# A cached-attention and MLP block on one core: wider filler matmuls, the first head's values on GpSimd's DMA queue, and a last output tile in three column parts

## The chip, the cores and the metric

The kernel runs on one core of one Trainium2 chip. The metric is the device time of one execution in microseconds, lower is better. The number for the kernel before is the median of six runs.

## The reference, cut to what matters

The input x has 2048 rows (tokens) of 640 columns. There are 32 heads with cached keys and values of 2048 positions and 128 columns each, all in bfloat16.

```python
mod = silu(c) @ w_mod                 # six vectors of 640: sa, ca, ga, sb, cb, gb
h   = layernorm(x) * (1 + ca) + sa
q   = h @ wq                          # 32 heads of 128
p   = softmax(q @ k_cache.T / sqrt(128))
x   = x + ga * ((p @ v_cache) @ wo)
h   = layernorm(x) * (1 + cb) + sb
u   = gelu(layernorm(h) @ w1)         # four column groups, shifted by +1, -1, +2, -2 rows
x1  = h + shifted(u) @ w2
h2  = gelu(layernorm(x1) @ w3) @ w4   # 1728 hidden columns
out = x + gb * (x1 + h2)
```

## The kernel before, in words

The tokens are cut into four chunks of 512 and the heads into eight groups of four. Attention is 128 steps. A step takes one chunk and one head: 16 score matmuls of 128x512 (L806), eight exponentials on ScalarE of 128x1024 each (L808), and 64 matmuls of 128x129 against the values (L825, the 129th column sums the exponentials). While a step runs, TensorE also makes the next step's queries (`q_proj`, L729), and after four heads of a chunk it multiplies by wo (`wo_group`, L760). Then a tail does the MLP in tiles: `w1_part` (L940), `w2_tile` (L963), `w3_part` (L989) and `w4_tile` (L1002 and after). The order of the tail is written out by hand in the list `TAIL`. Its last entry is D15, `w4_tile` of the last 128 rows.

The order of instructions on each engine is made by a planner in Python (class `Plan`). Each operation has a cost in nanoseconds, a priority, and the operations that it depends on. TensorE follows the priorities strictly. The other engines are filled by the planner's clock. `after=` gives only an order in the planner; the program has no wait for it. `reads` and `writes` become semaphore waits. The planner's own figures are not times of the chip.

Before the first step there is a head of some 13 us:

- POOL fills `ones` (L403) and an identity, and the 129th columns of five value buffers (`v_ones`, L410).
- SP loads the row c, two tiles of x, three of the five parts of w_mod's first 1280 columns (`wm[0]`, `wm[2]`, `wm[4]`, L434) and the first head's slice of wq. ACT's queue loads the other two tiles of x, `wm[1]` and `wm[3]`, and, later, another slice of wq.
- TensorE runs filler matmuls on `ones` (`spin` and `dummy`, L440): 30, then it turns c into a column (`spread`, L452), then 26 more. Then come 5 times 10 matmuls of one column (`mcol`, L465), one set per part of w_mod, which give sa and ca. In the first two sets a filler follows each matmul.
- The four normalised tiles of x are turned by TensorE (L586), scaled by ca and sa into `hT` on DVE (L595, k = 0, 2, 4) and ACT (L590, k = 1, 3), and multiplied by wq (L729). Three more groups of fillers (8, 9 and 9) lie around this.
- The first head's keys K0 come by four transposing DMAs on SP (L610); the first waits for `wm[0]`, the others for `wm[2]`. The first head's values V0 come in two halves of 256 KB on ACT's queue (L677), which the planner puts behind the second pair of small activations, L504 and L505. POOL's queue then brings the second chunk of x (L562, it waits for the first `hT` of ACT), a slice of wq (L619, it waits for the second exponential) and the values V1, V2, V3 (L616; V1 waits for the third exponential).

At the end, `w4_tile` of D15 makes two halves of 320 columns: 14 matmuls, a multiplication by gb and an addition on DVE, and an output DMA for each half. The first half's outputs leave while the second half is computed.

Each engine's program ends in a second block of instructions, `fast`, that is reached by a branch. DVE takes its last six operations there and SP its last five (`FIRST`).

Of the kernel before, what the change touches and what calls it, by code (L numbers as in the profile page):

```python
# [6 lines left out]
ACT = mybir.ActivationFunctionType  # L7
# [33 lines left out]
class Plan:  # L41
# [50 lines left out]
    def schedule(self):  # L92
        for o in self.ops:
            for d in o.need:
                o.deps[d()] = True
            pre = set(o.deps) | o.order
            for d in pre:
                d.succ.append(o)
            o.ndep = len(pre)
        t_eng = {e: 0.0 for e in self.ENG}  # L100
        dma_t = {e: 1600.0 for e in self.ENG}
        avail = {e: [] for e in self.ENG}
        for o in self.ops:
            if o.ndep == 0:
                avail[o.eng].append(o)
        self.seq = {e: [] for e in self.ENG}
        free = {p: [] if p in self.late else [(0.0, b, ()) for b in range(len(bk))] for p, bk in self.pools.items()}
        left = {t: len(t.refs) for o in self.ops for t in o.newps}
        self.busy = {e: 0.0 for e in self.ENG}
        self.all = []  # L110
        pe = sorted((o for o in self.ops if o.eng == "PE"), key=lambda o: (o.prio, o.seq))
        pe_i = 0
        port = {"POOL": 0.0, "DVE": 0.0}
        while len(self.all) < len(self.ops):
            best = None
            for e in self.ENG:
                st = []
                for o in avail[e]:
                    if e == "PE" and o is not pe[pe_i]:
                        continue  # L120
                    r = o.ready
                    if not all(free[t.pool] for t in o.newps):
                        continue
                    r = max([r] + [min(free[t.pool])[0] for t in o.newps])

                    x = port["POOL" if e == "DVE" else "DVE"] if o.dual else 0.0
                    st.append((max(r, t_eng[e], x), o.prio, o.seq, o))
                if not st:
                    continue
                lim = min(st)[0] + 30.0  # L130
                c = min((x for x in st if x[0] <= lim), key=lambda x: x[1:3])
                if best is None or c[0] < best[0]:
                    best = c
            assert best is not None, ("stuck", pe[pe_i].prio, [d.eng for d in pe[pe_i].deps if not hasattr(d, "end")])
            s, o = best[0], best[3]
            e = o.eng
            avail[e].remove(o)
            if e == "PE":
                pe_i += 1
            for t in o.newps:  # L140
                b = min(free[t.pool])
                free[t.pool].remove(b)
                t.bank, t.ap = b[1], self.pools[t.pool][b[1]]
                for d in b[2]:
                    o.deps.setdefault(d, False)
            o.start = s
            if o.dual:
                port[e] = s + o.dur
            t_eng[e] = s + (o.dur if o.dma else max(o.dur - self.LAP.get(e, 0.0), 60.0))
            self.busy[e] += o.dur  # L150
            if o.dma:
                t = max(dma_t[e], s + o.dur)
                both = min(max(0.0, max(dma_t[x] for x in self.ENG if x != e) - t), o.kb * 1024 / 190.0)
                dma_t[e] = t + both + (o.kb * 1024 - 190.0 * both) / 380.0
                o.end = dma_t[e] + 2000.0
            else:
                o.end = s + o.dur + o.lat
            o.idx = len(self.seq[e])
            self.seq[e].append(o)
            self.all.append(o)  # L160
            for pool, bank in o.gives:
                free[pool].append((o.end, bank, (o,)))
            for u in o.succ:
                u.ndep -= 1
                u.ready = max(u.ready, (o.start if o not in u.deps else t_eng[e] + 45.0 if e == u.eng and e != "PE" and not o.dma and not u.deps[o] else o.end) + u.slack - (45.0 if e == u.eng and e in self.LAP and not o.dma else 0.0) + (1500.0 if o.dma and u.eng in ("DVE", "ACT") and not u.dma else 0.0))
                if u.ndep == 0:
                    avail[u.eng].append(u)
            for t in o.ptiles:
                left[t] -= 1
                if left[t] == 0:  # L170
                    last = {}
                    for r in t.refs:
                        if r.eng not in last or r.idx > last[r.eng].idx:
                            last[r.eng] = r
                    free[t.pool].append((max(r.end for r in t.refs), t.bank, tuple(last.values())))
        self.total = max(o.end for o in self.ops)
# [103 lines left out]
def fast_path(nc, es, flag, A_x, A_k_cache, A_v_cache, A_wq, A_wo, B_w1, B_w2, B_w3, B_w4, c, w_mod, out):  # L280
    _, SQ, D = A_x.shape
# [3 lines left out]
    KT, NKT, HD, QC, NC = D // 128, SK // 128, D // 2, 512, SQ // 512  # L285
    NF = (FF + 127) // 128
# [15 lines left out]
    P = Plan()  # L302
    T = lambda ap=None: Tile(ap)
# [24 lines left out]
    mod_t = {p: sb("mod%d" % p, [128, D], F32) for p in (2, 3, 4, 5)}  # L328
# [67 lines left out]
    def dma(eng, fn, kb, reads, writes, prio, need=(), after=(), over=()):  # L396
        return P.op(eng, fn, {"SP": 480, "ACT": 480, "POOL": 1000}[eng], reads, writes, prio, dma=True, kb=kb, need=need, after=after, over=over)
# [39 lines left out]

    def dummy(e, n, t=None):
        for _ in range(n):
            ins = e.matmul((t or warm)[:, 0:128], ones_t[:], ones_t[:], start=True, stop=True)  # L440
        return ins

    def spin(n, key, pool=None):
        t = Tile(pool=pool) if pool else warm
        P.op("PE", lambda e: dummy(e, n, t), n * 56, (ones,), (t,), key)

    mc, c_ps = Tile(pool="M"), Tile(pool="M")
    spin(30, -300)

    def spread(e):  # L450
        for k in range(KT):
# [6 lines left out]
    P.op("DVE", lambda e: e.reciprocal(c_e.ap, c_e.ap), 190, (c_e,), (c_e,), -300)  # L458
    P.op("DVE", lambda e: e.tensor_mul(out=c_f.ap, in0=c_e.ap, in1=c_ps[:, 0:KT]), 170, (c_e, c_ps), (c_f,), -300)
    P.op("DVE", lambda e: e.tensor_copy(s_bf.ap, c_f.ap), 170, (c_f,), (s_bf,), -300)  # L460
    spin(26, -298)
    for k in range(KT):
        def mcol(e, k=k):
            for j in range(2 * KT):
                ins = e.matmul(mc[:, j:j + 1], wm_ap[:, k, j * 128:(j + 1) * 128], s_bf[:, k:k + 1],  # L465
                               start=(k == 0 and j == 0), stop=(k == KT - 1), skip_group_check=True)
                if k < 2:
                    dummy(e, 1)
            return ins
        P.op("PE", mcol, 2 * KT * (85 if k < 2 else 62), (wm[k], s_bf, ones), (mc,) + ((warm,) if k < 2 else ()), -290 + k, accum=True)  # L470
    saT, caT = T(small(KT)), T(small(KT))
    P.op("DVE", lambda e: e.tensor_copy(saT.ap, mc[:, 0:KT]), 170, (mc,), (saT,), -290)
    P.op("DVE", lambda e: e.tensor_scalar_add(out=caT.ap, in0=mc[:, KT:2 * KT], scalar1=1.0), 170, (mc,), (caT,), -290)
# [200 lines left out]
            dma("SP", lambda e, n=n, p=p: e.dma_start(mod_t[p][:], m_scr.ap()[n:n + 1, :].to_broadcast([128, D])), 320, lines, tuple(mod[p]), slot + 1.0)  # L674

    for a, z, t in ((0, NKT // 2, v0a), (NKT // 2, NKT, V[0])):
        dma("ACT", lambda e, a=a, z=z: e.dma_start(V_ap[0][:, a:z, 0:128], A_v_cache[0, 0, a * 128:z * 128].rearrange("(t p) d -> p t d", p=128)),  # L677
            256, (), (t,), -296.5, after=(ln0[1],))

    def load_head(h):  # L680
# [103 lines left out]
    def step(s):  # L784
# [3 lines left out]
        q = QT[s % 3]  # L788
        gs = (g * NC + ch) % 2
        if s == 0:  # L790
            spin(8, -271)
            q_proj(0, [-270 + kk for kk in range(KT)])
            spin(9, -100, "O0")
            spin(9, 1.5, "O1")
        if s + 1 < NS:
            q_proj(s + 1, [NP * s + ((1.375, 1.3845)[kk] if kk < 2 and 0 < s < NS - NC * HG else 2.3) + 0.01 * (kk if kk > 1 else 0) + 0.0001 * kk for kk in range(KT)])
        o = [Tile(pool="O0"), Tile(pool="O1")]
# [119 lines left out]
    w4b = T()  # L917
# [77 lines left out]
    def w4_tile(t, key):  # L995
# [1 line left out]
        b = xb[t]  # L997
        m = Tile(pool="W")
        last = t == SQ // 128 - 1
        for hf in range(2):  # L1000
            for f in range(NF):
                P.op("PE", lambda e, f=f, hf=hf: e.matmul(m[:, hf * 512:hf * 512 + HD], gT_ap[:, f, i * 128:(i + 1) * 128],  # L1002
                                                                 w4_ap[f][:, hf * HD:(hf + 1) * HD], start=(f == 0), stop=(f == NF - 1)),
                     MM(HD), (gT[f], w4_of(f), w4b, pad2), (m,), key + hf + 0.01 * f, accum=True)
            if last:
                c0, c1 = hf * HD, (hf + 1) * HD
                w, o_ = tmp[t % 2], xin[3 * hf]
                P.op("DVE", lambda e, hf=hf, c0=c0, c1=c1: e.tensor_tensor(out=w[:, c0:c1], in0=m[:, hf * 512:hf * 512 + HD], in1=mod_t[5][:, c0:c1], op=ALU.mult),
                     490, (m, mod[5][hf]), (w,), key - 1000)
                P.op("DVE", lambda e, o_=o_, c0=c0, c1=c1: e.tensor_tensor(out=o_[:, c0:c1], in0=w[:, c0:c1], in1=b[:, c0:c1], op=ALU.add), 490, (w, b), (o_,), key)  # L1010
                dma("SP", lambda e, o_=o_, c0=c0, c1=c1: e.dma_start(out2d[t * 128:(t + 1) * 128, c0:c1], o_[:, c0:c1]), 80, (o_,), (), key)
        if last:
            return
# [780 lines left out]
```

## Time and profile before

| what | value |
|---|---|
| median of 6 runs | 1369.86 us (1368.31 to 1370.2) |
| the profiled execution's own time | 1370.22 us |
| its span | 1368.9 us |
| TensorE busy | 1362.0 us (99%) |
| ScalarE busy | 1103.2 us (81%) |
| VectorE busy | 574.7 us (42%) |
| GpSimd busy | 111.7 us (8%) |
| DMA, the whole span | 90.38 MB, mean 66 GB/s |
| chain that ended last | TensorE 98%, DMA 1%, DVE 1% |
| first exponential starts | 14.12 us |
| last matmul ends | 1366.06 us |

The span is the time from the first to the last recorded instruction; 1.32 us of the profiled execution's own time lie outside it. "Busy" adds the time in which an engine has at least one instruction under way. The fillers count as busy, so a TensorE that is 99% busy says little about the first microseconds: there one has to ask which of the matmuls are work.

### The profile page before, as it was taken

The page shows a single profiled execution, that of the slowest core. Times are in us where ns is not written, and L with a number is a line of the kernel's source. Part 1 is how long each engine was busy: PE and PEld are TensorE (multiplying, and loading weights), DVE is VectorE, ACT ScalarE, POOL GpSimd, SP SyncE. Part 2 cuts the span into 40 slices and gives each one's busy share as a digit, 9 for nine tenths or more (in the row PEclk, how much of TensorE's full clock was granted, in tenths as well). Part 3 has the DMA queues.
Part 4 walks back from the last instruction along what each step waited for, and adds up shares of the span by engine and source line. Part 5 has one row for each costly group of instructions (what it writes and reads, how often), then busy time and mean ns, then how long its engine had stood idle before and what let it go on. Part 6 is the DMA issues. An engine that isn't in the chain of part 4 may idle for free.

```text
span 1368.9 us, 29865 instructions
## 1 busy us (share of the span) xinstructions
PE 1362.0 (99%) x13075; PEld 939.8 (69%) x13075; DVE 574.7 (42%) x1440; ACT 1103.2 (81%) x1145; POOL 111.7 (8%) x97
## 2 busy tenths in 40 slices
PE   9999999999999999999999999999999999999999
PEld 6676777777777777767777777767776776655665
DVE  5554344445332332332333233233233345799553
ACT  6988888888888888888888888888888888833322
POOL 1000000000000000000000000000233237500000
PEclk9999999999999999999999999999999999999999
DMA  9752614272325221241205121522236110441210
GB/s 214 140 98 38 114 41 79 35 128 59 83 63 90 55 48 36 51 88 30 58 10 101 36 47 36 91 54 48 55 61 139 26 17 17 114 84 44 41 43 31
DMA packets 264787, 90.38 MB, mean 66 GB/s; under 512 B 244793, under 2 KB 262266, under 8 KB 264650
## 3 DMA queue, kind: packets, MB, share of 16 engines
q1 hardware_dynamic: 260682, 84.17, 31.2%
q0 software_dynamic: 672, 2.56, 0.9%
q10 hardware_dynamic: 3296, 1.67, 0.6%
q8 instruction: 104, 1.70, 0.5%
q14 instruction: 33, 0.27, 0.1%
HBM read 41.68 MB, written 2.63 MB: 32 GB/s over the span
## 4 chain that ended last, share of the span: by engine, by line
PE 98%; DMA 1%; DVE 1%; issue 0%; ACT 0%; POOL 0%; POOLq 0%; ACTq 0%
PE f_O L825 34%; PE f_S L806 32%; PE f_M L729 10%; PE f_M L760 10%; PE f_S L1002 2%; PE f_M L1002 2%; PE f_O L989 2%; PE f_S L989 2%; PE f_S L940 1%; PE f_S L963 1%; PE f_M L963 1%; DMA f_KV<-in_A_v_cache_dram 1%; PE f_O L940 1%; PE f_S L440 1%; PE f_O L760 0%
## 5 line engine op out<-in xcount | busy, mean ns | idle before, releaser
L808 ACT ACTIVATE f_PQ<-f_S 128x1024 bf16<-128x1024 f32 x1024 | 1042.6, 1024 | 137.8 <-PE f_S L806 124.8
L825 PEld LDWEIGHTS f_O<-f_KV,f_PQ 128*128 128x128 bf16 x8192 | 634.8, 98 | 262.3 <-DVE f_small L517 1.4
L825 PE MATMUL f_O<-f_KV,f_PQ 128*128 128x129 bf16 x8192 | 796.4, 220 | 1.0 <-DMA f_KV<-in_A_v_cache_dram 0.9
L806 PE MATMUL f_S<-f_PQ,f_KV 128*128 128x512 bf16 x2048 | 721.5, 379 | 1.4 <-DMA f_KV<-in_A_k_cache_dram 1.0
L768 DVE TENSOR_TENSOR f_y<-f_M,f_y 128x320 f32<-128x320 f32 x192 | 94.5, 492 | 465.6 <-PE f_M L760 465.6
L760 PE MATMUL f_M<-f_wo,f_OO 128*128 128x320 bf16 x992 | 272.9, 299 | 0.0
L806 PEld LDWEIGHTS f_S<-f_PQ,f_KV 128*128 128x128 bf16 x2048 | 191.6, 98 | 13.6 <-ACT f_PQ L808 2.4
L729 PE MATMUL f_M<-f_hT,f_wq 128*128 128x512 bf16 (+1 forms) x640 | 189.9, 378 | 0.3 <-DVE f_tmp L771 0.2
L760 PEld LDWEIGHTS f_M<-f_wo,f_OO 128*128 128x128 bf16 x992 | 96.3, 98 | 28.5
L834 DVE TENSOR_TENSOR f_OO<-f_O,f_rl 128x256 bf16<-128x256 f32 x256 | 108.3, 423 | 8.3
L538 POOL TENSOR_TENSOR f_y<-f_y,f_mod 128x640 f32<-128x640 f32 x32 | 49.2, 1543 | 735.0 <-DVE f_y L768 734.9
L733 DVE CAST f_PQ<-f_M 128x512 bf16<-128x512 f32 x127 | 87.7, 691 | 50.8 <-PE f_M L729 50.6
L729 PEld LDWEIGHTS f_M<-f_hT,f_wq 128*128 128x128 bf16 x640 | 62.5, 98 | 50.4 <-ACT f_hT L590 0.7
L832 DVE RECIPROCAL f_rl<-f_O 128x2 f32<-128x2 f32 x256 | 43.5, 170 | 68.7 <-PE f_O L825 57.1
L992 ACT ACTIVATE f_OO<-f_S 128x512 bf16<-128x512 f32 x28 | 16.7, 597 | 43.6 <-PE f_S L989 43.6
L766 DVE COPY f_y<-f_M 128x320 f32<-128x320 f32 x32 | 15.7, 492 | 57.6 <-PE f_M L760 57.6
L499 DVE BATCH_NORM_STATS2 f_small<-f_y 128x6 f32<-128x320 f32 (+1 forms) x72 | 32.3, 479 | 1.4 <-POOL f_y L538 0.9
L1002 PE MATMUL f_M<-f_KV,f_OO 128*128 128x320 bf16 x224 | 31.7, 299 | 0.0
L1002 PE MATMUL f_S<-f_KV,f_OO 128*128 128x320 bf16 x224 | 31.7, 299 | 0.0
L544 ACT ACTIVATE f_xn<-f_y,f_small 128x640 bf16<-128x640 f32 x10 | 9.1, 915 | 25.7 <-DVE f_small L523 25.7
L661 DVE TENSOR_REDUCE f_small<-f_tmp 128x1 f32<-128x640 f32 x20 | 16.4, 820 | 29.7 <-ACT f_PQ L808 29.7
L992 ACT ACTIVATE f_OO<-f_O 128x512 bf16<-128x512 f32 x28 | 16.7, 596 | 14.1 <-PE f_O L989 14.1
(148 smaller groups left out, 538.5 us busy)
## 6 DMA issues: line engine op xcount, KB each, us to landing
f_KV<-in_A_v_cache_dram SPq DMA_DIRECT2D x28, 512.0 KB, 4.6
f_wo<-in_A_wo_dram SPq DMA_DIRECT2D x8, 640.0 KB, 4.2
f_wq<-in_A_wq_dram SPq DMA_DIRECT2D x7, 640.0 KB, 4.8
f_xin<-in_A_x_dram SPq DMA_DIRECT2D x13, 320.0 KB, 3.5
out_dram<-f_xin SPq DMA_DIRECT2D x15, 160.0 KB, 1.8
f_KV<-in_B_w_dram SPq DMA_DIRECT2D x5, 432.0 KB, 3.6
f_KV<-in_A_k_cache_dram SPq DMA_TRANSPOSE x128, 2.6
f_OO<-f_OO SPq DMA_TRANSPOSE x128, 2.5
```

The lines of the kernel that those rows point to most:

```text
L538: P.op(eng, lambda e: e.tensor_tensor(out=out, in0=a, in1=b, op=op), COST[eng][0], rd, wr, prio, lat=300 if eng == "POOL" else None, dual= ...
L729: P.op("PE", lambda e, i=i, kk=kk, mm=mm, a=a, z=z: e.matmul(mm[:, 0:z - a], wq_t[g % 2][:, kk, hh * 128:(hh + 1) * 128], hT_t[ch][:, kk, ...
L733: P.op("DVE", lambda e: e.tensor_copy(q.ap, m.ap), 690, (m,), (q,), s * NP - 90)
L760: P.op("PE", lambda e, m=m, qt=qt, hf=hf, hh=hh: e.matmul(m[:, 0:HD], OT_ap[gs][:, qt, hh, :], wo_t[g % 2][:, hh, hf * HD:(hf + 1) * HD], ...
L768: P.op("DVE", lambda e, m=m, yt=yt: e.tensor_tensor(out=yt.ap, in0=m[:, 0:HD], in1=yt.ap, op=ALU.add), 490, (m, yt), (yt,), s * NP - 60)
L806: P.op("PE", lambda e, sp=sp, r=r, kt=kt: e.matmul(sp[:, r * QC:(r + 1) * QC], K_ap[b][:, kt * 128:(kt + 1) * 128], q.ap, start=True, stop ...
L808: x = P.op("ACT", lambda e, sp=sp, pt=pt: e.activation(pt.ap.rearrange("p k q -> p (k q)"), sp.ap, ACT.Exp, scale=SCALE), 1021, (sp,), (pt ...
L825: ins = e.matmul(o[bk][:, w * 129:w * 129 + 129], pt[:, r, qt * 128:(qt + 1) * 128], V_ap[b][:, u, 0:129], start=(u == 0 and w == 0), stop ...
L832: P.op("DVE", lambda e, ov=ov, i0=i0: e.reciprocal(rl_t[:, i0:i0 + 2].unsqueeze(2), ov[:, 0:258].rearrange("p (u d) -> p u d", u=2)[:, :, ...
L834: evac.append(P.op("DVE", lambda e, ov=ov, i0=i0, bk=bk: e.tensor_tensor(out=On_ap[gs][:, 2 * bk:2 * bk + 2, hh, :], in0=ov[:, 0:258].rear ...
L989: P.op("PE", lambda e, m=m, f=f, kk=kk: e.matmul(m.ap, w3_ap[:, kk, f * 128:(f + 1) * 128], nT_ap[ch][:, kk, :], start=(kk == 0), stop=(kk ...
L1002: P.op("PE", lambda e, f=f, hf=hf: e.matmul(m[:, hf * 512:hf * 512 + HD], gT_ap[:, f, i * 128:(i + 1) * 128], w4_ap[f][:, hf * HD:(hf + 1) ...
```

## The change

Three things are changed, and a line of the planner. Fillers have 512 columns (the 128 columns of `ones` read four times over), and there are fewer of them: 8, 7, 2, 2 and 2 in place of 30, 26, 8, 9 and 9, and in the first two sets of `mcol` one after every fourth matmul. V0's two loads are issued by POOL. Output tile D15 is made in parts of 320, 192 and 128 columns; the third has a bank of its own from pool T.

```diff
-            t_eng[e] = s + (o.dur if o.dma else max(o.dur - self.LAP.get(e, 0.0), 60.0))
+            t_eng[e] = s + (o.dur if o.dma or e == "PE" else max(o.dur - self.LAP.get(e, 0.0), 60.0))
...
-            ins = e.matmul((t or warm)[:, 0:128], ones_t[:], ones_t[:], start=True, stop=True)
+            ins = e.matmul((t or warm)[:, 0:512], ones_t[:], ones_t[:].unsqueeze(1).to_broadcast([128, 4, 128]), start=True, stop=True)
...
-        P.op("PE", lambda e: dummy(e, n, t), n * 56, (ones,), (t,), key)
+        P.op("PE", lambda e: dummy(e, n, t), n * 216, (ones,), (t,), key)
...
-    spin(30, -300)
+    spin(8, -300)
...
-    spin(26, -298)
+    spin(7, -298)
...
-                if k < 2:
+                if k < 2 and j % 4 == 3:
                     dummy(e, 1)
...
     for a, z, t in ((0, NKT // 2, v0a), (NKT // 2, NKT, V[0])):
-        dma("ACT", lambda e, a=a, z=z: e.dma_start(V_ap[0][:, a:z, 0:128], ...
+        dma("POOL", lambda e, a=a, z=z: e.dma_start(V_ap[0][:, a:z, 0:128], ...
             256, (), (t,), -296.5, after=(ln0[1],))
...
-            spin(8, -271)
+            spin(2, -271)
             q_proj(0, [-270 + kk for kk in range(KT)])
-            spin(9, -100, "O0")
-            spin(9, 1.5, "O1")
+            spin(2, -100, "O0")
+            spin(2, 1.5, "O1")
...
-        for hf in range(2):
+        if last:
+            m3 = Tile(pool="T")
+            parts = ((m, 0, 0, HD), (m, 512, HD, 512), (m3, 0, 512, D))
+        else:
+            parts = ((m, 0, 0, HD), (m, 512, HD, D))
+        for n, (mm, o, c0, c1) in enumerate(parts):
             for f in range(NF):
...
-                     MM(HD), (gT[f], w4_of(f), w4b, pad2), (m,), key + hf + 0.01 * f, accum=True)
+                     MM(c1 - c0), (gT[f], w4_of(f), w4b, pad2), (mm,), key + n + 0.01 * f, accum=True)
             if last:
-                c0, c1 = hf * HD, (hf + 1) * HD
-                w, o_ = tmp[t % 2], xin[3 * hf]
+                w, o_ = tmp[t % 2], xin[(0, 3, 1)[n]]
...
                 dma("SP", lambda e, o_=o_, c0=c0, c1=c1: e.dma_start(out2d[t * 128:(t + 1) * 128, c0:c1], o_[:, c0:c1]), 80, (o_,), (), key)
```

The order of the instructions follows from the source and the planner. Against the kernel before, ACT's and POOL's orders differ only by V0's two loads: on POOL they stand straight behind the memsets of L410, and the first of them waits for those memsets alone. On DVE one query cast moves ahead of a few statistics in the early steps. DVE's block `fast` now holds the six operations of the three parts, so that the two operations of the tile before it stand ahead of the branch. SP's block `fast` holds the last five output DMAs as before, now two whole tiles and three parts. V1's load on POOL now also waits for a semaphore of V0's first half.

More of the change, by code (lines that the diff above doesn't have):

```diff
@@ L466, in mcol @@
                                start=(k == 0 and j == 0), stop=(k == KT - 1), skip_group_check=True)
-                if k < 2:
+                if k < 2 and j % 4 == 3:
                     dummy(e, 1)
             return ins
-        P.op("PE", mcol, 2 * KT * (85 if k < 2 else 62), (wm[k], s_bf, ones), (mc,) + ((warm,) if k < 2 else ()), -290 + k, accum=True)
+        P.op("PE", mcol, 2 * KT * (72 if k < 2 else 62), (wm[k], s_bf, ones), (mc,) + ((warm,) if k < 2 else ()), -290 + k, accum=True)
     saT, caT = T(small(KT)), T(small(KT))
@@ L676, in fast_path @@
     for a, z, t in ((0, NKT // 2, v0a), (NKT // 2, NKT, V[0])):
-        dma("ACT", lambda e, a=a, z=z: e.dma_start(V_ap[0][:, a:z, 0:128], A_v_cache[0, 0, a * 128:z * 128].rearrange("(t p) d -> p t d", p=128)),
+        dma("POOL", lambda e, a=a, z=z: e.dma_start(V_ap[0][:, a:z, 0:128], A_v_cache[0, 0, a * 128:z * 128].rearrange("(t p) d -> p t d", p=128)),
             256, (), (t,), -296.5, after=(ln0[1],))
@@ L999, in w4_tile @@
         last = t == SQ // 128 - 1
-        for hf in range(2):
+        if last:
[4 more added lines that the diff above has]
+        for n, (mm, o, c0, c1) in enumerate(parts):
             for f in range(NF):
-                P.op("PE", lambda e, f=f, hf=hf: e.matmul(m[:, hf * 512:hf * 512 + HD], gT_ap[:, f, i * 128:(i + 1) * 128],
-                                                                 w4_ap[f][:, hf * HD:(hf + 1) * HD], start=(f == 0), stop=(f == NF - 1)),
-                     MM(HD), (gT[f], w4_of(f), w4b, pad2), (m,), key + hf + 0.01 * f, accum=True)
+                P.op("PE", lambda e, f=f, mm=mm, o=o, c0=c0, c1=c1: e.matmul(mm[:, o:o + c1 - c0], gT_ap[:, f, i * 128:(i + 1) * 128],
+                                                                             w4_ap[f][:, c0:c1], start=(f == 0), stop=(f == NF - 1)),
+                     MM(c1 - c0), (gT[f], w4_of(f), w4b, pad2), (mm,), key + n + 0.01 * f, accum=True)
             if last:
-                c0, c1 = hf * HD, (hf + 1) * HD
-                w, o_ = tmp[t % 2], xin[3 * hf]
-                P.op("DVE", lambda e, hf=hf, c0=c0, c1=c1: e.tensor_tensor(out=w[:, c0:c1], in0=m[:, hf * 512:hf * 512 + HD], in1=mod_t[5][:, c0:c1], op=ALU.mult),
-                     490, (m, mod[5][hf]), (w,), key - 1000)
-                P.op("DVE", lambda e, o_=o_, c0=c0, c1=c1: e.tensor_tensor(out=o_[:, c0:c1], in0=w[:, c0:c1], in1=b[:, c0:c1], op=ALU.add), 490, (w, b), (o_,), key)
+                w, o_ = tmp[t % 2], xin[(0, 3, 1)[n]]
+                P.op("DVE", lambda e, mm=mm, o=o, c0=c0, c1=c1: e.tensor_tensor(out=w[:, c0:c1], in0=mm[:, o:o + c1 - c0], in1=mod_t[5][:, c0:c1], op=ALU.mult),
+                     dve(c1 - c0), (mm,) + tuple(mod[5]), (w,), key - 1000)
+                P.op("DVE", lambda e, o_=o_, c0=c0, c1=c1: e.tensor_tensor(out=o_[:, c0:c1], in0=w[:, c0:c1], in1=b[:, c0:c1], op=ALU.add),
+                     dve(c1 - c0), (w, b), (o_,), key)
                 dma("SP", lambda e, o_=o_, c0=c0, c1=c1: e.dma_start(out2d[t * 128:(t + 1) * 128, c0:c1], o_[:, c0:c1]), 80, (o_,), (), key)
```

## The prediction

> **What bounds the kernel now.** I read the page first: chain by engine, then the windows of the first microseconds, the timeline of the head, the DMA issues, and the timeline of the end. The chain is TensorE for 98% of the span; all the rest of the kernel's idle time lies in the head and behind the last matmul.
>
> ```profile
> PE 98%; DMA 1%; DVE 1%; issue 0%; ACT 0%; POOL 0%; POOLq 0%; ACTq 0%
> ```
>
> So between about 28 us and the last matmul nothing in the change can help or hurt: no matmul of work is added, and the orders are the same but for one query cast. What moves the time is when the steps get going, and what follows the last matmul. The chain of waits of the first 35 us names what is there: fillers, `mcol`, the transposes, then a piece of ACT's queue, then V1's load.
>
> ```profile
> 4.61 2.54 PE f_S L440 x26
> ...
> 11.04 0.02 ACTq L252
> 11.05 0.05 issue
> 11.11 0.79 ACT f_hT L590
> ...
> 17.27 10.16 DMA f_KV<-in_A_v_cache_dram
> ```
>
> The timeline shows why ACT begins its first `hT` at 11.11 though the transposes were ready at about 10.45 (DVE's first `hT` starts there): ACT's queue was issuing V0's two loads from 8.93 to 11.00.
>
> ```profile
> 8.93 2.07 ACTq L677 DMA_DIRECT2D f_KV<-in_A_v_cache_dram  x2
> 11.11 0.78 ACT L590 ACTIVATE f_hT<-f_O,f_small 128x512 bf16<-128x512 bf16 x1 [1.98 <-DVE f_hT L595]
> ```
>
> The windows show the other resource (the stretch, its length, busy time and instructions of TensorE, its weight loads, DVE, ACT and POOL, then granted clock, busy share of the DMA engines and GB/s).
>
> ```profile
> 2.00:4.00 2.00, 2.00 (x22) 2.00 (x20) 0.11 (x1) 1.28 (x1) 0.00 (x0) 1.00 0.92 303
> 4.00:6.00 2.00, 2.00 (x23) 1.79 (x22) 1.50 (x8) 0.18 (x1) 0.00 (x0) 1.00 1.05 407
> 6.00:8.00 2.00, 2.00 (x40) 2.00 (x39) 2.00 (x8) 0.41 (x2) 0.00 (x0) 1.00 1.04 401
> 10.00:12.00 2.00, 1.90 (x25) 1.20 (x23) 1.62 (x6) 0.89 (x2) 0.00 (x0) 1.00 1.37 75
> 24.00:28.00 4.00, 2.10 (x15) 1.08 (x16) 2.62 (x14) 2.20 (x3) 1.15 (x1) 1.00 1.25 146
> ```
>
> From 3 to 8 us the DMA engines are full at some 400 GB/s with x, w_mod and wq. These loads are needed at once. The issue rows taken load by load give: `wm[0]` issued at 1.65, landing 5.2 later, at 6.85; `mcol` starts at 6.93. `wm[4]` issued at about 2.6, landing 6.4 later, at 9.0; its matmuls start at about 9.1. There is 0.1 us of slack in each.
>
> **V0 on POOL, the ACT side.** ACT no longer issues two loads, so `hT` k = 1 can start with the transposes' end, 10.5 in place of 11.11, and k = 3 at 11.25 in place of 11.78. The last query matmul waits for k = 3 (ends 12.55): it would come at 12.03, with DVE's k = 4 (ends 11.9) just behind. Gain 0.55 us.
>
> **V0 on POOL, the DMA side.** POOL's last memset ends at 1.87 and nothing else holds V0, so it is issued at 1.9, two issues of about 0.95 each (rows: 0.86, 0.96 and 1.15 to 1.19 for POOL's others). Between POOL's issue of x at 12.19 and the first packets of its queue at 15 lay some 2.8 us, so V0 moves between about 4 and 8 us, into the full stretch. It puts nothing new on DMA in all, but puts 0.52 MB ahead of w_mod. Price: V3 on this same queue took 20.1% of 16 engines over 9 us, 1.81 us; at the 407 GB/s of large rows it would be 1.29; at the 256 GB/s that V0's own 256-byte rows made at 12 to 13 us, 2.05. I take 1.8, the same data on the same queue. `wm[4]` then lands at 10.8, the last `mcol` ends at 11.1 in place of 9.45, and the 20 transposes (1.05 us) and all behind them shift by 1.7. The tiles of x are delayed too (the second pair from 5.67 to at most 7.5), but from there four half-tile statistics and two sums (2.1), ACT's small pair (0.4) and two normalisations (0.75) end at 10.75, before 11.1. The bounds: if V0 came too late to pass `wm[4]`, 0; at 256 GB/s, 2.0.
>
> The rows do not show how three queues share the engines. If they went by order of issue, V0's second half (issued at 2.85) would come behind `wm[4]` (2.6), and the price would be half, 0.9: that lies within the bounds. The Trainium skill's "DMA: Bandwidth & Descriptors", section "Queues, rings and completion order", speaks against this part: each DMA engine takes turns between the queues that have work, packet by packet. By that rule V0 is never behind `wm[4]` and the whole 1.8 is charged, so that the sum would be +0.65 by the rule and -0.25 by the order of issue.
>
> Queued behind V0 on POOL are x chunk 1, wq and V1. They wait for ACT's `hT` and exponentials anyway and follow them, by the same shift; V1's added semaphore belongs to a load that landed long before. In place of 9 to 15.7 us, V0 no longer meets K0's transposes, which then have room: K0's first part, issued when `wm[0]` lands (8.65), needs at most the 5.6 us it took, 14.2, and is used at 13.47 + 1.15 = 14.6. Covered by 0.4.
>
> **From there to 28 us.** Shift of the first exponential: +1.7 - 0.55 = +1.15. K1 (TensorE waited 0.98 for it) is released by the first exponential, V1 (0.94) by the third, so both carry the shift. They may come relatively earlier because x chunk 1 no longer meets V0's last packets (15.7): between 0 and 0.5, I take 0.15. Net +1.0 at 28 us, and ScalarE and TensorE are busy from there on, so it stays.
>
> **Fillers.** Cold, 30 of them took 3.38 us; eight of four times the columns take 8 x 0.43 = 3.4 (0.107 spacing of 128 columns, times four). The second group: its spacing falls from 0.107 to 0.056 at about 6.5 us; 7 wide ones end between 7.0 and 7.6 in place of 6.97. With `wm[0]` at 8.65 both are hidden; without that cover they would cost 0 to 0.6. In `mcol`, 20 pairs at 0.081 = 1.62 become 20 x 0.028 + 4 x 0.216 = 1.42, hidden behind `wm[2]` and `wm[4]`. The other groups are 0.43 in place of 0.45 to 0.50. Zero in all; the planner's line likewise (orders unchanged).
>
> **The last tile.** The timeline of its end:
>
> ```profile
> 1366.09 0.49 DVE L1008 TENSOR_TENSOR f_tmp<-f_S,f_mod 128x320 f32<-128x320 f32 x1 [0.89 <-PE f_S L1002]
> 1366.62 0.49 DVE L1010 TENSOR_TENSOR f_xin<-f_tmp,f_y 128x320 bf16<-128x320 f32 x1
> ```
>
> A 320-column DVE operation takes 0.49, a 640-column one 0.82: 0.16 + 0.00103 per column, so 0.295 for 128 and 0.36 for 192. Matmuls: 14 of 320 take 1.90 (0.1357 each), 128 columns 0.056, so 192 is 0.082: 14 x (0.082 + 0.056) = 1.93, +0.03. The second part's pair (0.75) ends about when the third part's matmuls (0.78) do. Then 0.295 + 0.295 + 0.04 in place of 1.02: DVE ends 0.36 earlier. The last DMA is smaller (32 KB in place of 80 KB; 1.6 to landing), gain 0 to 0.2, I take 0. SP's third issue (0.4) fits into the 0.7 between the parts. One new exposure: DVE's branch into its last block now falls in the 0.22 us pause before the first part, where before it had 1.26; unseen, 0 to 0.9, I take 0 since part one has 0.1 more to spare. Tail: -0.35.
>
> **Sum.** +1.0 - 0.35 = +0.65 on the profiled execution's 1370.22 gives 1370.9. That execution is 0.36 above the median of the runs (1369.86), so the median I forecast is 1370.5. What a measurement can tell from no change is about 0.2%, 2.7 us: this is inside. Its own range, from the bounds (0 to 2.0 for w_mod, 0 to 0.6 for fillers, -0.5 for V1, 0.9 and -0.2 at the tail): -0.55 - 0.5 - 0.55 = -1.6 to 2.0 - 0.55 + 0.6 - 0.35 + 0.9 = +2.6, or 1368.3 to 1372.5. Chance 0.56.
>
> **Rival, slower: TensorE falls back to its slow rate.** Matmuls were paced at 0.107 per 128 columns until 6.5 us, at 0.056 after, and the granted clock in the rows (1.00 throughout) does not show this. With `wm[0]` at 8.65 TensorE idles some 1.5 us, then in short pieces until 11.1. If that undoes the faster rate and 5.5 us of steady work are again needed, the transposes cost +1.05, the first scores +0.4, the queries of step two ahead of the third pair of scores +1.1, the rest of the queries and values +0.6: +3.2, total +3.8, 1373.7. It decides where a wait of that length falls in a stretch that switches. Against it: in 24 to 28 us TensorE was busy 2.10 of 4.00, and the pair of score matmuls at 28.02 still took 0.59, as before. The Trainium skill's "TensorE: Matmul & The Clock Gate", section "What's actually happening", has the clock halve after an idle window of about 3.4 us; by that rule a 1.5 us wait costs nothing, no run here shows where the limit lies. Chance 0.32 for this and other lateness beyond 1372.6.
>
> **Rival, faster: V0 passes without delaying w_mod, and K1 and V1 come in time.** Then -0.55 at ACT, -0.98 and -0.94 of TensorE's two waits, -0.35 at the tail: -2.8, 1367.0. For it: DMA from 20 to 28 us moves under 150 GB/s, so it is stalls, not bytes, that make K1 and V1 late, and stalls shift. Against it: the full stretch from 3 to 8 us. Chance 0.12, nearly all beyond 0.2% since only the whole of it is this case.
>
> **Rival: the three parts do nothing,** since the output DMA's fixed time is what ends last: then +1.0, 1370.9. It lies within the forecast's range.
>
> **How the numbers follow.** Faster 0.12, same 0.56, slower 0.32. The range takes the forecast's own and most of the slow rival: 1368.0 to 1374.0; left out are the fast case and the end of the slow one.
>
> **What would show it.** Right: V0's packets on GpSimd's queue before 8 us; `mcol`'s last set about 1.7 later; ACT's first `hT` straight behind the transposes; first exponential at about 15.3; DVE's last operation ending 0.66 behind the last matmul's end. Wrong: `mcol` ending before 10; matmuls of 128 columns at 0.107 after 9 us; a first exponential before 14; K1 or V1 waits much different from 0.98 and 0.94.

## The result, and the profile after

The changed kernel takes 1373.95 us (median of 16 runs, 1372.33 to 1375.36), the kernel before beside it 1369.88 (36 runs, 1367.68 to 1372.46). The ratio is 1.0029, interval 1.0023 to 1.0036: slower by 4 us. The time lies within the predicted range (1368.0 to 1374.0), 0.05 us under its upper end. The likeliest case (1370.5) did not come, and the forecast's own bounds (1368.3 to 1372.5) did not hold it either: it lies in the range only because the range was widened for the rival that was called slower. That rival came, at nearly its total (1373.7), but not by its sizes, so the nearness is luck.

The profiled execution of the changed kernel took 1373.89 us, with a span of 1372.5 against 1368.9 before. Its chain by engine has lost one per cent from TensorE to DMA:

```profile
PE 97%; DMA 2%; DVE 1%; issue 0%; ACT 0%; SPq 0%; POOL 0%; POOLq 0%; DVEq 0%
```

The chain of waits over the first microseconds (start, length, what) shows which DMA. Before, fillers stood here; now it is w_mod's fifth part, issued at 2.61 and landing at 11.52, and then `mcol`'s last set.

```profile
2.61 8.91 DMA f_W<-in_w_mod_dram
11.57 0.41 PE f_M L465 x10
...
13.86 0.79 ACT f_hT L590
```

The issues of the DMA view confirm it (KB each, microseconds to landing): 6.4 for `wm[4]` before (first line), 8.9 now, and 7.3 for the first half of V0, which was issued at 1.96.

```profile
f_W<-in_w_mod_dram SPq DMA_DIRECT2D x1, 320.0 KB, 6.4
...
f_W<-in_w_mod_dram SPq DMA_DIRECT2D x1, 320.0 KB, 8.9
f_KV<-in_A_v_cache_dram POOLq DMA_DIRECT2D x1, 256.0 KB, 7.3
```

The queues of the DMA view between 6 and 8 us show when V0 moves (packets, MB, share of 16 engines). `q0` is GpSimd's queue. It moved nothing before 6 us; then 0.24 of V0's 0.52 MB went beside the last of w_mod and wq.

```profile
q0 software_dynamic: 60, 0.24, 41.8%
q1 hardware_dynamic: 102, 0.24, 36.3%
q10 hardware_dynamic: 102, 0.22, 28.2%
```

The timeline shows what TensorE does with it (the bracket: idle time before, and what ended it). `mcol`'s third and fourth sets wait 1.37 us, the last set 1.06. The first exponential starts at 17.31, before 14.12.

```profile
9.86 0.65 PE L465 MATMUL f_M<-f_s_bf,f_W 128*128 128x1 bf16 x20 [1.37 <-DMA f_W<-in_w_mod_dram]
11.57 0.41 PE L465 MATMUL f_M<-f_s_bf,f_W 128*128 128x1 bf16 x10 [1.06 <-DMA f_W<-in_w_mod_dram]
...
13.75 0.54 DVE L595 TENSOR_SCALAR f_hT<-f_O,f_small 128x512 bf16<-128x512 bf16 x1 [1.50 <-PE f_O L586]
13.86 0.78 ACT L590 ACTIVATE f_hT<-f_O,f_small 128x512 bf16<-128x512 bf16 x1 [4.53 <-PE f_O L586]
...
17.31 2.85 ACT L808 ACTIVATE f_PQ<-f_S 128x1024 bf16<-128x1024 f32 x3 [0.70 <-PE f_S L806]
```

And the windows (stretch, length, busy time and instructions of TensorE, weight loads, DVE, ACT and POOL, then granted clock, DMA share and GB/s) show what follows the waiting. The clock column read 1.00 in every stretch of the head before. Now it reads 0.50 from 12 to 14 us. In shorter stretches it is 1.00 until about 11.68 and again from about 15.1: 3.4 us at half clock.

```profile
8.00:10.00 2.00, 0.63 (x14) 0.43 (x13) 1.97 (x8) 0.41 (x2) 0.00 (x0) 1.00 1.02 262
10.00:12.00 2.00, 0.94 (x32) 0.85 (x30) 0.24 (x1) 0.00 (x0) 0.00 (x0) 0.92 1.21 246
12.00:14.00 2.00, 2.00 (x21) 2.00 (x20) 0.48 (x3) 0.14 (x1) 0.00 (x0) 0.50 1.26 236
```

The last tile's end, from the timeline and the DMA issues of the changed kernel. DVE ends 0.73 behind the last matmul (1369.36), but the small output DMAs land 2.5 and 2.2 us after their issue, where the halves before took 1.6:

```profile
1368.42 0.94 PE L1008 MATMUL f_O<-f_KV,f_OO 128*128 128x128 bf16 x14
...
1369.80 0.29 DVE L1015 TENSOR_TENSOR f_xin<-f_tmp,f_y 128x128 bf16<-128x128 f32 x1
```

```profile
out_dram<-f_xin SPq DMA_DIRECT2D x1, 48.0 KB, 2.5
out_dram<-f_xin SPq DMA_DIRECT2D x1, 32.0 KB, 2.2
```

### The profile page after: what moved, and what is told of

It reads as the page before. It is cut to its first block, busy times and chain, and to the rows that moved or that the text cites. A ratio compares the mean times of both kernels' runs of the same rounds, so it can differ in the third digit from the quotient of the medians.

```text
span 1372.5 us, 29744 instructions
## 1 busy us (share of the span) xinstructions
PE 1362.6 (99%) x13012; PEld 936.3 (68%) x13012; DVE 574.6 (42%) x1442; ACT 1103.3 (80%) x1145; POOL 113.4 (8%) x99
## 3 DMA queue, kind: packets, MB, share of 16 engines
q10 hardware_dynamic: 1216, 1.15, 0.3%
HBM read 41.68 MB, written 2.63 MB: 32 GB/s over the span
## 4 chain that ended last, share of the span: by engine, by line
PE 97%; DMA 2%; DVE 1%; issue 0%; ACT 0%; SPq 0%; POOL 0%; POOLq 0%; DVEq 0%
PE f_O L825 33%; PE f_S L806 31%; PE f_M L729 10%; PE f_M L760 10%; PE f_M L1008 2%; PE f_O L989 2%; PE f_S L989 2%; PE f_S L1008 2%; PE f_S L940 1%; PE f_S L963 1%; PE f_M L963 1%; DMA f_KV<-in_A_v_cache_dram 1%; DMA f_W<-in_w_mod_dram 1%; PE f_O L940 1%; DMA f_hT<-f_xn 0%
## 5 line engine op out<-in xcount | busy, mean ns | idle before, releaser
L808 ACT ACTIVATE f_PQ<-f_S 128x1024 bf16<-128x1024 f32 x1024 | 1042.6, 1024 | 137.9 <-PE f_S L806 124.9
L1008 PE MATMUL f_S<-f_KV,f_OO 128*128 128x320 bf16 (+1 forms) x224 | 31.0, 296 | 0.0
L1008 PEld LDWEIGHTS f_M<-f_KV,f_OO 128*128 128x128 bf16 x224 | 21.9, 98 | 8.9
```

The lines of the kernel that those rows point to most:

```text
L808: x = P.op("ACT", lambda e, sp=sp, pt=pt: e.activation(pt.ap.rearrange("p k q -> p (k q)"), sp.ap, ACT.Exp, scale=SCALE), 1021, (sp,), (pt ...
L1008: P.op("PE", lambda e, f=f, mm=mm, o=o, c0=c0, c1=c1: e.matmul(mm[:, o:o + c1 - c0], gT_ap[:, f, i * 128:(i + 1) * 128], w4_ap[f][:, c0:c1 ...
```

## The experiments

The theory after the result had two steps: V0's bytes on GpSimd's queue make w_mod late, and TensorE's waiting for it costs half the clock for a while. The rivals were that the lateness alone is the loss, that the fillers or the three parts have a share, and, in the first step, that it is V0's short rows and not its bytes.

### One part at a time

**The changed kernel with V0 back on ACT's queue.**

```diff
-        dma("POOL", lambda e, a=a, z=z: e.dma_start(V_ap[0][:, a:z, 0:128], ...
+        dma("ACT", lambda e, a=a, z=z: e.dma_start(V_ap[0][:, a:z, 0:128], ...
```

> The changed kernel with one part undone: V0's two loads are back on ACT's queue. Theory A (V0's bytes come ahead of w_mod): wm[2] and wm[4] land at about 8.1 and 9.0 us again, the first exponential starts at 14.1 to 14.4 us, the granted clock stays at 1.00, and the time is that of the kernel before, 1369.9, plus at most 0.3 from the tail. Theory B (the fewer, wider fillers leave TensorE idle and let its clock fall): the clock row still shows 0.50 somewhere between 8 and 15 us and the time stays above 1372.

Measured: ratio 1.0000 (0.9991 to 1.0009). `wm[4]` lands at 9.0, the clock in the profile is 1.00 throughout, the first exponential starts at 13.80. The loss is gone with this one line.

**V0 on POOL's queue alone.**

```diff
-        dma("ACT", lambda e, a=a, z=z: e.dma_start(V_ap[0][:, a:z, 0:128], ...
+        dma("POOL", lambda e, a=a, z=z: e.dma_start(V_ap[0][:, a:z, 0:128], ...
```

> The kernel before with one part of the change: V0's two loads on GpSimd's queue, old fillers, old last tile. Theory A: wm[4] lands at about 11.5 us, the first exponential comes 2.5 to 3.2 us late, and the time is 1372.5 to 1374. Theory B: the old fillers between mcol's matmuls keep TensorE's clock at 1.00 and the time is at most 1371.

Measured: ratio 1.0033 (1.0020 to 1.0046), as much as the whole change. `mcol` waits 0.74, 1.24 and 0.86; the first exponential starts at 17.40. Its windows have the same fall of the clock, so the wide fillers have nothing to do with it:

```profile
10.00:12.00 2.00, 1.02 (x32) 0.94 (x33) 0.02 (x1) 0.00 (x0) 0.00 (x0) 0.95 1.92 247
12.00:14.00 2.00, 2.00 (x23) 2.00 (x21) 0.42 (x3) 0.08 (x1) 0.00 (x0) 0.50 0.57 111
```

**The three column parts alone.**

```diff
-        for hf in range(2):
+        if last:
+            m3 = Tile(pool="T")
+            parts = ((m, 0, 0, HD), (m, 512, HD, 512), (m3, 0, 512, D))
```

> The kernel before with one part of the change: the last output tile in parts of 320, 192 and 128 columns. By the prediction's step: DVE's last operation ends 0.35 us earlier after the last matmul and so does the span, 1369.5. By the changed kernel's trace: the last DMA needs 0.6 us longer from issue to landing, which eats the gain, 1370.1 (+0.2). Theory A and B say nothing of it.

Measured: 1.0006 (0.9997 to 1.0015). No gain that can be told; by the interval it is anything from a gain of 0.4 us to a loss of 2.1.

**The wide fillers and the planner's line alone.**

```diff
-            ins = e.matmul((t or warm)[:, 0:128], ones_t[:], ones_t[:], start=True, stop=True)
+            ins = e.matmul((t or warm)[:, 0:512], ones_t[:], ones_t[:].unsqueeze(1).to_broadcast([128, 4, 128]), start=True, stop=True)
```

> The kernel before with one part of the change: the fillers of 512 columns (and the planner's line), V0 on ACT's queue, old last tile. Theory A: nothing is late, 1369.6 to 1370.1, clock 1.00. Theory B: clock below 1.00 in the head and 1371 to 1373.

Measured: 1.0000 (0.9992 to 1.0009), with the first exponential at 13.80 and the clock at 1.00. The zero for the fillers held.

### The clock and the lateness apart

**V0 on POOL, and fillers where `mcol` waits.** The load is as late as before, but TensorE has matmuls of 128 columns to do meanwhile.

```diff
+        if k in (1, 3):
+            spin(22 if k == 1 else 14, -290 + k + 0.5)
...
-        dma("ACT", lambda e, a=a, z=z: e.dma_start(V_ap[0][:, a:z, 0:128], ...
+        dma("POOL", lambda e, a=a, z=z: e.dma_start(V_ap[0][:, a:z, 0:128], ...
```

> The kernel before with V0's loads on GpSimd's queue, and 22 and 14 more fillers of 128 columns behind the second and the fourth set of mcol, where TensorE waits for wm[2] and wm[4]. Theory A1 (the loss is the late w_mod and, on top, TensorE's clock falling while it waits): the clock stays 1.00, the 20 transposes take 1.1 us in place of 2.1, the first exponential comes at about 15.8 in place of 17.4, and the time is 1.3 to 1.8 us under that of the second experiment. Theory A2 (the late w_mod alone, the clock does not matter because ScalarE and DMA set the pace there): the time stays within 0.5 us of it.

Measured: 1.0009 (1.0000 to 1.0018) where V0 alone gave 1.0033 (1.0020 to 1.0046); the intervals do not meet, and the gain is more than the 1.3 to 1.8 us that were expected. The mean granted clock is 1.000 in all 11 runs; in V0 alone it was 0.997 to 0.999. `wm[4]` is no earlier: 9.2 us from issue to landing. The windows of this kernel, to be held against those of V0 alone:

```profile
8.00:10.00 2.00, 2.00 (x49) 2.00 (x48) 1.97 (x7) 0.41 (x2) 0.00 (x0) 1.00 1.03 264
10.00:12.00 2.00, 2.00 (x52) 1.96 (x49) 0.02 (x1) 0.00 (x0) 0.00 (x0) 1.00 1.18 264
12.00:14.00 2.00, 2.00 (x41) 1.83 (x40) 0.97 (x4) 0.68 (x2) 0.00 (x0) 1.00 2.43 135
```

The waits between the sets are filled, but one stays ahead of the first set, behind the old fillers:

```profile
7.74 0.18 PE L465 MATMUL f_M<-f_s_bf,f_W 128*128 128x1 bf16 x1 [1.59 <-DMA f_W<-in_w_mod_dram]
```

So filling the waits keeps the clock. It takes back about 0.0024 x 1370 = 3.3 us by the two ratios, give or take some 2 us by their intervals, but not all of that is shown to be the clock's own cost. The first exponential (16.50, expected 15.8) is only 0.90 earlier than with V0 alone; `mcol`'s last set starts 0.28 later there (11.91 for 11.63), so that some 1.2 us go to the clock. The larger part lies at 24 to 32 us, where TensorE stood idle 1.99 us with V0 alone and not at all here (0.77 us of it are lost again between 32 and 60 us). That hole also differs between kernels whose clock stayed at 1.00 (1.90 us in the kernel before, none in the first experiment), so a single profile does not tie it to the clock.

**V0 on POOL, but behind `wm[4]`.** It is issued when the last part of w_mod has landed.

```diff
-            256, (), (t,), -296.5, after=(ln0[1],))
+            256, (wm[4],), (t,), -296.5, after=(ln0[1],))
```

> The kernel before with V0's loads on GpSimd's queue, but waiting for wm[4], so that they leave ACT's queue and still do not come ahead of w_mod. Theory A: wm[4] lands at 9.0 to 9.1, ACT's first hT follows the transposes at about 10.6, the first exponential starts at 13.8, and the time is that of the kernel before or up to 0.5 us less. A rival that blames GpSimd's queue itself (slow or late issue, x chunk 1 and V1 held behind V0): the time is over 1371.

Measured: 1.0003 (0.9993 to 1.0012), V0 issued at 9.54, `wm[4]` landing in 6.6 us, clock 1.00, first exponential at 13.88. It is the early start on GpSimd's queue that costs, not the queue. An early start on another queue was not run. ACT's first `hT` starts at 10.71 against 11.11 before, but that bought nothing measurable.

### Bytes or rows

**The kernel before with one more load on POOL's queue at the start, 512 KB that nobody reads, in rows of 1024 bytes.** V0 stays on ACT's queue.

```diff
+    dma("POOL", lambda e: e.dma_start(spare_ap.rearrange("p (t d) -> p t d", t=4), x2d[0:512, 0:512].rearrange("(t p) d -> p t d", p=128)),
+        512, (), spare, -296.5)
```

> The kernel before, and one more load of 512 KB that nobody reads, on GpSimd's queue at the start, in rows of 1024 bytes; V0 stays on ACT. If bytes alone make w_mod late, wm[4] lands 1.3 us later (512 KB at 407 GB/s), at 10.3 us, and the same in the next experiment. If the short rows cost more, it lands 1.3 later here and 2.5 later there.

**The same in rows of 256 bytes, as V0 has.**

```diff
+    dma("POOL", lambda e: e.dma_start(spare_ap.rearrange("p (t d) -> p t d", t=16), A_v_cache[0, 0].rearrange("(t p) d -> p t d", p=128)),
+        512, (), spare, -296.5)
```

> The kernel before, and one more load of 512 KB that nobody reads, on GpSimd's queue at the start, in rows of 256 bytes as V0 has them; V0 stays on ACT. If bytes alone count, wm[4] lands 1.3 us later; if the short rows cost more, 2.5 us later, at 11.5, with the DMA engines moving about 265 GB/s in 8 to 10 us, and the time is 1371.5 to 1374.

Measured: 1.0014 (1.0004 to 1.0023) and 1.0034 (1.0021 to 1.0047). The issues of the DMA view, first of wide rows, then of short rows, have `wm[4]` 2.0 and 2.8 later than before:

```profile
f_W<-in_w_mod_dram SPq DMA_DIRECT2D x1, 320.0 KB, 8.4
```

```profile
f_W<-in_w_mod_dram SPq DMA_DIRECT2D x1, 320.0 KB, 9.2
```

Both are later than was expected (1.3 and 2.5). Most of the lateness is bytes, 0.8 of it is rows, by one profile each. From 6 to 12 us the packets of GpSimd's queue took 23.6% of the time of the 16 DMA engines with wide rows and 32.4% with short rows, which is 1.42 and 1.94 us of all engines: some 0.5 of the 0.8 is their own time. And `wm[4]` was later than that own time by 0.6 and 0.9. The 0.8 also parts the two profiles by their clock: with wide rows `mcol` waits 0.78 and 0.46 and the profile has 1.00 throughout; with short rows it waits 1.56 and 0.78, and the clock falls at about 12.4 for 3.4 us. The runs with wide rows are divided: four have a mean clock of 1.000 (1369.9 to 1372.1), six have 0.999 (1371.7 to 1372.9). That kernel lies on the edge.

### The last tile, cut otherwise

**Two parts, of 384 and 256 columns, and of 448 and 192,** each with one run, on the kernel before.

```diff
+            parts = ((m, 0, 0, 384), (m, 512, 384, D))
```

> The kernel before with the last output tile in two parts of 384 and 256 columns, so that the rows of the two output DMAs have 768 and 512 bytes. If it is rows under 512 bytes that make the three parts' last DMA slow to land, this one lands in 1.6 to 1.7 us as before, DVE's last two operations take 0.42 each in place of 0.49, and the stretch from DVE's first operation of the tile to the end of the span, 4.7 to 4.8 us before, shrinks by about 0.15, the first part being later by 0.4 but its work off the path. If it is the number of DMAs, likewise. One look: the time itself cannot show 0.15.

```diff
+            parts = ((m, 0, 0, 448), (m, 512, 448, D))
```

> The kernel before with the last output tile in two parts of 448 and 192 columns (rows of 896 and 384 bytes). If short rows make the last DMA slow to land, it takes 2.2 to 2.5 us from issue to landing; if the third DMA did it, 1.6 to 1.7. DVE's last two operations take 0.36 each. One look.

Measured: 1370.46 and 1369.44 in one run each, the kernel before beside them at a median of 1370.24: nothing can be told from the times. From the end of the last matmul to the end of the span it was 2.60 and 2.63, against 2.84 before. The issue row of 448 and 192:

```profile
out_dram<-f_xin SPq DMA_DIRECT2D x1, 48.0 KB, 1.5
```

**The changed kernel with V0 behind `wm[4]` and the last tile in 384 and 256.**

```diff
-            256, (), (t,), -296.5, after=(ln0[1],))
+            256, (wm[4],), (t,), -296.5, after=(ln0[1],))
...
-            parts = ((m, 0, 0, HD), (m, 512, HD, 512), (m3, 0, 512, D))
+            parts = ((m, 0, 0, 384), (m, 512, 384, D))
```

> The changed kernel with V0's loads waiting for wm[4] and the last tile in two parts of 384 and 256 columns: what the experiments so far would keep. Theory: wm[4] lands at 9.0 to 9.1, the first exponential starts at 13.8, the clock is 1.00, and the time is 0 to 0.5 us under the kernel before, which may be too little to tell.

Measured: median 1369.53, 1.0002 (0.9990 to 1.0015), with runs from 1368.25 to 1376.78. It can't be told from the kernel before. The profiled run is one of the long ones (span 1373.9), at a clock of 1.00: TensorE was busy only 10.14 us of 14 between 16 and 30 us, waiting for K1 (2.5 us in three waits) and for a slice of wq (1.3), and the output DMA of the last part took longer to land than in any other kernel; from the last matmul's end to the span's end it is 3.95:

```profile
out_dram<-f_xin SPq DMA_DIRECT2D x1, 64.0 KB, 2.8
```

## Why the prediction was right or wrong

**The place was right.** V0's move is the whole loss, the fillers alone are zero, and the head's lateness stays to the end: the last whole tile's first operation on DVE is 3.28 later (1365.57 for 1362.29), after 3.19 at the first exponential.

**V0 on POOL, the DMA side: the term was mis-sized.** It took 1.8; the measured lateness of `wm[4]` is 2.5. V0's own time, priced from V3's row, was about right: its packets took 32.6% of the 16 engines from 6 to 12 us, 1.96 us. What was missing is that `wm[4]` was later than the own time of the added packets, by 0.5 here and by 0.6 and 0.9 for the extra loads with wide and short rows; what makes that rest stays open. The bounds, 0 to 2.0, did not hold the value, since they counted only V0's own time on the engines. On the question of order, `wm[4]` was issued before V0's second half and the queue of V0 sent nothing until 6 us, and yet w_mod paid for all of V0's own time. That speaks for the Trainium skill's rule of "DMA: Bandwidth & Descriptors", "Queues, rings and completion order" (turns by packet between queues), and against the order of issue, which would have given 0.9.

**`wm[0]` at 8.65 was wrong.** It was the only wait the prediction had for TensorE, and TensorE began its first set of `mcol` at 6.97, as before, since V0's packets came too late to meet `wm[0]` (with V0 alone it was 7.08, with V0 held back 7.15 and 7.48; with fillers in `mcol` it was 7.74, in one profile each). The waits came between the sets instead, 1.37 and 1.06, which the prediction did not list. So the fillers were not covered as the prediction had it, and cost nothing all the same.

**The clock was the step that failed.** The forecast charged zero. In the changed profile the first transpose starts 2.48 later (11.84 for 9.36). The 20 transposes take 2.09 in place of 1.11, and the group of fillers behind them 0.85 in place of 0.58, as it does with the old fillers and V0 alone (0.86). The first two queries are slower too (0.42 and 0.32 where they took 0.28 and 0.27), but the ten queries together take 1.25 in place of 1.79, since they no longer wait for `hT`. So the first exponential: +2.48 for `mcol`'s last set, +0.98 and +0.27 for the clock, -0.54 for the queries, makes +3.19, as measured, where +1.15 was forecast.

How much of the 4 us at the end is the clock's is not settled. By the 18 runs of the changed kernel that have a clock on record, three with a mean clock of 1.000 took 1372.3 to 1372.8, nine with 0.999 took 1372.4 to 1374.5 (median 1373.9), two with 0.998 took 1372.7 and 1374.5, and four with 0.997 took 1374.6 to 1375.4. That leaves some 2.8 us without the fall and 1.2 for one fall, about as much as the profile has. But with fillers in `mcol`, where `wm[4]` was as late, only 1.2 us of loss are left. The stall at 24 to 32 us, which differs from profile to profile, may be in it; the clock's share stays open between 1.2 and 3.3 us.

**The slower rival had the mechanism and wrong sizes.** Its +1.05 for the transposes is nearly right (0.98). The scores (+0.4), most of the queries (+1.1) and the rest (+0.6) were not paid: the rival took 5.5 us of slow rate, the half clock lasted 3.4, so that the clock was back at 15.1 and the scores at 16.67 took their usual time. The w_mod term that it shared was 0.7 too low, and the tail was wrong in sign. The errors nearly cancel in the total, which is luck. Nor was the wait that it named, 1.5 us for `wm[0]`, the one that came. Its doubt was put in the right place: "no run here shows where the limit lies". Now runs show something of it. One wait of 1.59 us behind fillers, in the experiment with fillers in `mcol`, left the clock at 1.00. A stretch from 8.3 to 11.7 us with under 1 us of work, most of it one-column matmuls, brought it to 0.50. The Trainium skill's "TensorE: Matmul & The Clock Gate", "What's actually happening", names an idle window of about 3.4 us. Here the stretch held matmuls and two separate waits, neither as long as that (1.37 and 1.06), so a fall needs no unbroken gap of that length. How little work it takes is not settled: in the 3.4 us ahead of the fall TensorE was busy 0.98 us in the changed kernel, 1.30 with V0 alone and 1.14 with short rows, while in the last experiment 1.20 of 3.41 us, from 25.0 to 28.4, left the clock at 1.00. That work was matmuls of 129 to 512 columns, which may be the difference; no run tests it. The forecast took single waits of 1.5 us to be safe and charged nothing for two of them in a row.

**V0 on POOL, the ACT side, was right.** ACT's `hT` starts 0.11 behind DVE's, before 0.66.

**K1 and V1 were not constant.** The waits were 0.39 and 0.92 where 0.98 and 0.94 were carried. But TensorE's whole idle time from 17 to 60 us is 2.03 (0.25, 0.39, 0.92 and 0.47 in four stretches) where it was 1.92; among the rest is 0.3 for a late `hT` of the second chunk. The relief of 0.15 that was forecast came out at nothing: 3.28 at the end after 3.19 at the first exponential.

**The last tile: -0.35 became +0.30.** DVE's part was right (0.73 behind the last matmul, forecast 0.66, before 1.05). Its branch, given 0 to 0.9, cost nothing that shows: the pause ahead of the first part is 0.22, as before. The gain was lost in the DMAs behind. From the last matmul's end to the span's end it is 2.80 to 2.97 in the seven kernels with two halves (2.84 before), and 3.14, 3.29 and 2.82 in the three kernels with three parts. The rival that the parts do nothing was nearer. "The last DMA is smaller, gain 0 to 0.2" failed: the parts of 48 KB took 2.4 to 2.9 to landing, those of 32 KB 1.9 to 2.4. It isn't the short rows of 384 bytes alone, since those landed in 1.5 as the second of two parts, and a part of 64 KB in 512-byte rows took 1.5 in one profile and 2.8 in another. What sets it stays open.

## What to carry to other kernels

A load that is needed later should not be issued early beside loads that are needed now, however idle its queue is: let it wait for the last urgent load to land, as the experiment with V0 behind `wm[4]` did. When a load gets later, ask what the waiting engine does meanwhile: here a TensorE that had only one-column matmuls and waits for some 3.4 us paid again, at half clock for the next 3.4 us, and fillers in the waits (not only ahead of them) prevented that. Price a smaller last output from the landing times of several profiles, not from the compute time ahead of it.

## What the runs showed of the hardware

The half clock lasted the same 3.4 us in three kernels (11.7 to 15.1, 11.8 to 15.2 and 12.4 to 15.8), though TensorE was busy throughout by then. The first packets of GpSimd's queue came some 4.5 us after V0's issue at 1.96 (none before 6.4); the prediction took 2.8 from another issue, and put V0 from 4 us on. ACT's issue of the same two loads of V0 took from 1.02 to 2.14 us in different kernels (2.07 in the kernel before), so that the 0.55 us of relief there is not in every version. And between 24 and 32 us TensorE stood idle for 1.90 us in the kernel before, for none in the first experiment and in the wide fillers alone:

```profile
16.00:30.00 14.00, 14.00 (x150) 9.87 (x149) 9.56 (x38) 13.18 (x15) 3.21 (x3) 1.00 1.10 228
```

This is the window from 16 to 30 us of the first experiment, with TensorE busy for all of it; yet its ratio to the kernel before, run beside it, is 1.0000. So the stalls at K1 and V1 in one profile need not stand for all runs of a kernel, and a forecast should not count on their removal.
